# Decoding of all weight tiles but the first waits for the eighth pair's queries, and two more gates use Silu

## The chip, the cores and the metric

The kernel runs on one core of a Trainium2 chip. TensorE multiplies, VectorE and ScalarE work element by element, GpSimd does a little on the side, and SyncE issues the transfers. The metric is the device time of one execution in microseconds (us), as the median of several runs.

## What is computed

The inputs are q, k, v of 8 batches and 8 heads (576 tokens of 64 values), a projection to 128 features, and three weight matrices, which arrive as 64-bit floats. Linear attention comes first, a gated feed-forward over all 4608 tokens behind it:

```python
def phi(x):
    proj = np.einsum('bhsd,df->bhsf', x, w_phi)
    proj = proj - np.max(np.abs(proj), axis=-1, keepdims=True)
    return np.concatenate([np.exp(proj), np.exp(-proj)], axis=-1)
q_p, k_p = (phi(q), phi(k))
kv = np.einsum('bhsf,bhsd->bhfd', k_p, v)
z = np.sum(k_p, axis=2)
num = np.einsum('bhsf,bhfd->bhsd', q_p, kv)
den = np.einsum('bhsf,bhf->bhs', q_p, z)[..., None] + 1e-06
x = (num / den) ...                     # (4608, 512)
g = x @ w_gate                          # (4608, 1536)
silu = g * (1.0 / (1.0 + np.exp(-g)))
val = x @ w_val
return (silu * val @ w_out)
```

## The kernel before

The attention works on 32 pairs of heads, one after the other (`attention(i, rank)`). For each pair the keys are projected by TensorE, centred by VectorE (L498, L503), put through the exponential by ScalarE and multiplied with the values. The queries of the first eight pairs, the early ones, are projected, centred in three pieces (a maximum at L622, a subtraction at L627, whose three results are kept in `last["qm", n]`, n = 3i to 3i+2), turned on TensorE (L637) and exponentiated (L644). Their results are split into a rounded part and a remainder, `xh` and `xl` (L783, L785), the operands of the feed-forward. The sums of keys and values are copied by ScalarE at L561.

The feed-forward's inner width of 1536 is cut into 12 weight tiles f, the tokens into column tiles c of 384. For a weight tile and a column tile, `first` makes gate and value in two banks `gv` with 24 matmuls of 128x384 (4 blocks of the contraction, gate and value, 3 products of split operands), and `second` multiplies the result with w_out, 9 matmuls of 128x512. Weight tile after weight tile meets the first three column tiles, since these are done first; the products of column tiles 2 and 3 are stored and multiplied with w_out later. `first` makes the gate in two ways. With Tanh, ScalarE reads the gate's bank and VectorE reads it again (L878) before it multiplies with the value (L881). With Silu, ScalarE alone reads the gate's bank (L869), and VectorE makes one instruction (L872). Which one is taken is set by `SILU`, a half-open range of pairs (f, c).

The weights are decoded by `weight_piece`, once for the gate and value columns of a tile (`layer` 0, 128x1024, tiles named `a` or `spare`) and once for its rows of w_out (`layer` 1, 128x512, tiles named `spare` or `m`). A piece is loaded into one of three buffers. ScalarE takes the magnitude of the high words (L383), VectorE makes six steps of bit work and arithmetic (L384, L386, L389, L392, L394, L397), ScalarE rounds (L399), and VectorE makes the remainder (L400). The buffer of the raw words is free again after the fifth of VectorE's steps (L394). In the third buffer, `spare`, lie the w_out rows of tiles 0 and 1, and then the gate and value columns of tiles 3, 5, 7 and so on; gate and value columns of tiles 0, 1, 2, 4, 6 use the first.

The order of the instructions on all engines comes from a planner (`Plan`), which runs the steps in a model of the five engines when the program is built: each step has a cost, the steps that it follows, and a rank, and an engine that is free takes the ready step of the lowest rank. Attention of pair i has rank i, the feed-forward -1, the decoding 5 for the first piece and 7.12 to 7.33 for the others. When TensorE has nothing ready in the model, the planner writes a fill matmul on zeros (L1499 early, L1502 once a w_out sum is open), which it costs at 200 ns. On the chip every engine follows the written order.

Of the kernel before, what the change touches and what calls it, by code (L numbers as in the profile page):

```python
# [10 lines left out]
F32 = mybir.dt.float32  # L11
F32R = mybir.dt.float32r
U32 = mybir.dt.uint32
AF = mybir.ActivationFunctionType
# [13 lines left out]
NFT = DFF // P  # L28
# [16 lines left out]
EARLY_PAIRS = 8  # L45

W_RANKS = [5 if u == 0 else 7.125 if u == 1 else 7.1 + 0.01 * u for u in range(2 * NFT)]
SILU = (1, 0), (NFT - 3, 2)

EARLY = 3  # L50
PAIRS = 4
# [19 lines left out]
class Plan:  # L71
# [18 lines left out]
    def add(self, eng, cost, fn, after=(), rank=0.0, take=None, give=None):  # L90
        s = Step(eng, cost, fn, rank, len(self.steps), self.LAG[eng], take, give, (rank, len(self.steps)))
        seen = set()
        for a in after:
            if a is not None and id(a) not in seen:
                seen.add(id(a))
                a.then.append(s)
                s.left += 1
        s.early = self.early
        self.steps.append(s)
        return s  # L100
# [99 lines left out]
def dve(n):  # L200
    return 150 + 1.04 * n


def dve2(n):
    return 150 + 0.52 * n
# [6 lines left out]
def act(n):  # L212
    return 190 + 0.86 * n
# [11 lines left out]
def favor_attention_moe(ctx: ExitStack, tc: tile.TileContext, qT, kT, v, w_phi, wg, wv, wo, out):  # L225
    nc = tc.nc
# [13 lines left out]
    def sb(name, shape, dtype=F32, n=None):  # L240
        if n is None:
            return pool.tile(shape, dtype, name=name, tag=name)
        return [pool.tile(shape, dtype, name=f"{name}{i}", tag=f"{name}{i}") for i in range(n)]
# [52 lines left out]
    qm, qu = sb("qm", [P, 2 * NBL]), sb("qu", [P, 2 * NBL])  # L296
# [51 lines left out]
    add = plan.add  # L348
# [13 lines left out]
    raw_free, we_free, wa_free = [None] * 3, [None] * 3, [()] * 3  # L362

    def weight_piece(f, layer, rank, over):

        vec, n = nc.vector, (2 - layer) * DM
        u = (1 if f >= MORE else 2) if layer else (2 if f > MORE and f % 2 else 0)
        if f == MORE and layer:
            raw_free[1] = over
        first_ = lambda t: get(t)[:, :n]  # L370
        r = lambda: get((raw1, raw2, raw3)[u])[:, :2 * n].rearrange("p (n t) -> p n t", t=2)
        x, e = (lambda: first_((wa1, wa2, wa3)[u])), (lambda: first_((we1, we2, we3)[u]))
        low, high = (lambda: r()[:, :, 0]), (lambda: r()[:, :, 1])
        bits = lambda t: t.bitcast(U32)
        t = w1[f % W1_SETS]
        hi, lo = (w2_hi[f], w2_lo[f % W2_SETS]) if layer else (t[:, :, 0], t[:, :, 1])
        out_ = lambda x: x if layer else x.rearrange("p (u c) -> p u c", u=4)
        sets = (W1_SETS, W2_SETS)[layer]
        free = lo_user[layer][f - sets] if f >= sets else ()
        loads = [add("SP", (SLOW if f < 1 else INPUT) * P * DM * 8, lambda m=m, src=src: nc.sync.dma_start(  # L380
            get((raw1, raw2, raw3)[u])[:, 2 * DM * m:2 * DM * (m + 1)], src.bitcast(U32)), [raw_free[u]], rank)
            for m, src in enumerate([wo[f * P:(f + 1) * P]] if layer else [wg[f], wv[f]])]
        s0 = add("ACT", act(n), lambda: nc.scalar.activation(e(), high().bitcast(F32), AF.Abs), [*loads, we_free[u]], rank)  # L383
        s1 = add("DVE", dve2(n), lambda: vec.tensor_scalar(  # L384
            out=e(), in0=e(), scalar1=F64_LEAST, scalar2=F64_MOST, op0=ALU.max, op1=ALU.min), [s0], rank)
        s2 = add("DVE", dve2(n), lambda: vec.tensor_scalar(  # L386
            out=bits(e()), in0=bits(e()), scalar1=3, scalar2=0x3FFFFFFF, op0=ALU.logical_shift_left, op1=ALU.bitwise_and),
                 [s1], rank)
        s3 = add("DVE", dve(n), lambda: vec.scalar_tensor_tensor(  # L389
            out=bits(x()), in0=high(), scalar=0xC0000000, in1=bits(e()), op0=ALU.bitwise_and, op1=ALU.bitwise_or),  # L390
            [s2, *wa_free[u]], rank)
        s4 = add("DVE", dve2(n), lambda: vec.tensor_scalar(  # L392
            out=bits(e()), in0=bits(x()), scalar1=0xFF800000, scalar2=None, op0=ALU.bitwise_and), [s3], rank)
        s5 = add("DVE", dve(n), lambda: vec.scalar_tensor_tensor(  # L394
            out=e(), in0=low(), scalar=2.0**-52, in1=e(), op0=ALU.mult, op1=ALU.mult), [s4], rank)
        raw_free[u] = s5
        s6 = add("DVE", dve(n), lambda: vec.tensor_tensor(out=x(), in0=x(), in1=e(), op=ALU.add), [s5], rank)  # L397
        we_free[u] = s6
        s7 = add("ACT", act(n), lambda: nc.scalar.copy(hi, out_(x())), [s6, *(() if layer else free)], rank)  # L399
        s8 = add("DVE", dve(n), lambda: vec.tensor_tensor(out=lo, in0=out_(x()), in1=hi, op=ALU.subtract),  # L400
                 [s7, *free], rank)
        wa_free[u] = [s8]
        w_ready[f, layer] = [s7, s8]
        if not layer:
            w_stored[f, 4] = add("SP", P * n * 4, lambda: nc.sync.dma_start(w1_whole[f], x()), [s6], rank)
            wa_free[u].append(w_stored[f, 4])
        if layer:
            w_stored[f, layer] = add("SP", P * n * 4, lambda: nc.sync.dma_start(w2_dram[f], lo.bitcast(F32)), [s8], rank)
            w_stored[f, 4 + layer] = add("SP", P * n * 4, lambda: nc.sync.dma_start(w2_whole[f], x()), [s6], rank)
            wa_free[u].append(w_stored[f, 4 + layer])  # L410
        else:
            store = lambda x, f=f, t=t: w_stored.update({(f, 0): add("SP", P * n * 8, lambda: nc.sync.dma_start(
                w1_dram[f, :, :4], t.rearrange("p u h c -> p u (h c)").bitcast(F32)), [s8, x], rank)})
            if f:
                while later:
                    later.pop()(s8)
                store(None)
            else:
                later.append(store)
        if f == NFT - 1:  # L420
            weights_done.append(s8)
# [12 lines left out]
    last = {}  # L434
# [403 lines left out]
    def first(c, f, low):  # L838
# [28 lines left out]

        if c < EARLY and SILU[0] <= (f, c) < SILU[1]:
            s1 = add("ACT", act(CH), lambda: nc.scalar.activation(get(t_), ps_gv[0][:, :CH], AF.Silu),  # L869
# [90 lines left out]
    for f in range(NFT):  # L960
        for layer in range(2):
            weight_piece(f, layer, W_RANKS[2 * f + layer], over)
        low = parts_of_weights(f, 0, w_ready[f, 0])
        for c in range(EARLY):
            if c == EARLY - 1 and f == NFT - 1:
                put_off()
            j, h = first(c, f, low)
            if c:
                keep(c, f, j, h)
            else:  # L970
                put_off(0, f, parts(j, h), parts_of_weights(f, 1, w_ready[f, 1]))
# [40 lines left out]
    s0, s1_ = ((set2 + n) % X_SETS for n in (1, 2))  # L1012
# [541 lines left out]
```

## Time and profile before

| | |
|---|---|
| time, median of 3 runs (lowest, highest) | 1138.6 us (1135.88, 1138.96) |
| profiled execution: time, span | 1135.21 us, 1133.3 us |
| TensorE clock granted, mean | 0.997 |
| busy: TensorE, VectorE, ScalarE, GpSimd | 99%, 78%, 55%, 9% |
| TensorE on the chain that ended last | 88% |

The span goes from the first to the last instruction. Busy shares are means over stages of different kinds: the early pairs of heads with the decoding between them up to about 107 us, the twelve weight tiles for three column tiles beside the rest of the decoding to about 240 us, and after that the other pairs and column tiles.

### The profile page before, as it was taken

The numbers are of one execution on the slowest core, as the hardware profiler recorded it, in microseconds if no ns is written. First come the engines' busy times: TensorE is split into PE (matmuls) and PEld (weight loads), VectorE is DVE, ScalarE is ACT, GpSimd is POOL, SyncE is SP. The second block draws the span as 40 slices with busy tenths as digits, with TensorE's granted clock in tenths as the row PEclk, the third lists the DMA queues.
The fourth block names the chain that finished last, engine by engine and source line by source line (L and its number), as shares of the span: only waits on it lengthen the run. The fifth ranks groups of instructions, "written<-read, shape, count | busy, mean of one in ns | idle before, by whom it ended". The sixth has DMA issues, their size and how long they took to land.

```text
span 1133.3 us, 28130 instructions
## 1 busy us (share of the span) xinstructions
PE 1116.4 (99%) x11185; PEld 1061.5 (94%) x11185; DVE 889.3 (78%) x1418; ACT 627.6 (55%) x1373; POOL 104.3 (9%) x192
## 2 busy tenths in 40 slices
PE   9998999999999999999999999999999999999998
PEld 8887999999888899999899999999999999999998
DVE  6989999888787878889888999858556567979663
ACT  6876433365667676676675765644334345444342
POOL 0000000012120222122101000000420000000000
PEclk9999999999999999999999999999999999999999
DMA  6656899754788887789888897689997888642511
GB/s 176 170 186 231 300 315 297 259 178 139 233 256 256 275 267 257 242 282 328 263 254 262 288 351 248 222 257 325 306 305 235 266 263 288 212 167 85 182 43 42
DMA packets 161554, 269.56 MB, mean 238 GB/s; under 512 B 56464, under 2 KB 106640, under 8 KB 158352
## 3 DMA queue, kind: packets, MB, share of 16 engines
q1 hardware_dynamic: 161120, 267.64, 72.4%
q8 instruction: 88, 1.44, 0.5%
q14 instruction: 42, 0.34, 0.1%
q10 hardware_dynamic: 304, 0.13, 0.0%
HBM read 187.50 MB, written 80.22 MB: 236 GB/s over the span
## 4 chain that ended last, share of the span: by engine, by line
PE 88%; DMA 4%; DVE 4%; ACT 1%; issue 1%; POOL 0%; ACTq 0%; SPq 0%; DVEq 0%; POOLq 0%
PE gv L357 18%; PE gv L1127 14%; PE o L1127 14%; PE o L357 9%; PE work L1374 7%; PE work L357 5%; PE gv L1374 5%; PE o L1374 5%; PE work L540 4%; PE work L727 4%; DMA w<-w_dram 2%; PE work L767 1%; PE work L549 1%; DMA a<-w_dram 1%; DMA w_dram<-a 1%
## 5 line engine op out<-in xcount | busy, mean ns | idle before, releaser
L357 PE MATMUL gv<-xh,w 128*128 128x384 f32 x768 | 212.6, 341 | 1.1 <-DVE m L878 0.6
L357 PEld LDWEIGHTS gv<-xh,w 128*128 128x128 f32 x768 | 140.2, 188 | 3.5 <-DVE m L878 1.1
L357 PE MATMUL gv<-xl,w 128*128 128x384 f32 x384 | 128.9, 336 | 0.0
L357 PE MATMUL o<-w_hi,hidden 128*128 128x512 f32 x288 | 102.7, 402 | 0.0
L1127 PE MATMUL gv<-xh,w 128*128 128x384 f32 x336 | 99.8, 340 | 2.5 <-DMA w<-w_dram 1.5
L1127 PE MATMUL o<-m,w 128*128 128x384 f32 x388 | 80.9, 336 | 0.3 <-ACT snap L1137 0.2
L357 PEld LDWEIGHTS gv<-xl,w 128*128 128x128 f32 x384 | 72.3, 188 | 1.0 <-DVE xl L785 0.3
L1127 PEld LDWEIGHTS o<-m,w 128*128 128x128 f32 x388 | 68.5, 188 | 1.0 <-ACT snap L1137 0.6
L1127 PEld LDWEIGHTS gv<-xh,w 128*128 128x128 f32 x336 | 61.8, 188 | 4.4 <-issue 3.0
L357 PEld LDWEIGHTS o<-w_hi,hidden 128*128 128x128 f32 x288 | 54.1, 188 | 10.9
L1140 DVE TENSOR_TENSOR snap<-o,snap 128x384 f32<-128x384 f32 x72 | 39.9, 555 | 28.3 <-PE o L1127 23.3
L1140 DVE TENSOR_TENSOR snap<-gv,snap 128x384 f32<-128x384 f32 x72 | 39.9, 554 | 26.7 <-PE gv L1127 18.4
L1137 ACT COPY snap<-gv 128x384 f32<-128x384 f32 x72 | 34.3, 476 | 42.8 <-PE gv L1127 26.6
L357 PE MATMUL o<-w_lo,hidden 128*128 128x512 f32 x144 | 56.9, 395 | 0.0
L1137 ACT COPY snap<-o 128x384 f32<-128x384 f32 x72 | 34.2, 476 | 40.9 <-PE o L1127 25.2
L1127 PE MATMUL o<-xh,w 128*128 128x384 f32 x188 | 55.6, 341 | 1.0 <-DMA w<-w_dram 1.0
L1127 PE MATMUL gv<-xl,w 128*128 128x384 f32 x168 | 56.4, 336 | 0.0
L1147 ACT ACTIVATE m<-snap 128x384 f32<-128x384 f32 x47 | 24.7, 525 | 53.2 <-DVE snap L1140 47.5
L498 DVE TENSOR_REDUCE km<-work 128x4 f32<-128x512 f32 (+1 forms) x85 | 46.6, 548 | 8.8 <-PE work L357 8.6
L727 PE MATMUL work<-m,m 128*64 128x65 f32 x1664 | 53.4, 221 | 0.0
L727 PEld LDWEIGHTS work<-m,m 128*64 128x64 f32 x1664 | 51.0, 138 | 0.2 <-issue 0.2
L980 POOL TENSOR_TENSOR m<-m 128x256 f32<-128x256 f32 x48 | 38.6, 803 | 128.6 <-ACT m L528 26.3
(448 smaller groups left out, 3080.1 us busy)
## 6 DMA issues: line engine op xcount, KB each, us to landing
w<-w_dram SPq DMA_DIRECT2D x113, 512.0 KB, 5.6
h_dram<-m SPq DMA_DIRECT2D x90, 192.0 KB, 5.0
w_dram<-w SPq DMA_DIRECT2D x12, 1024.0 KB, 6.4
w_dram<-a SPq DMA_DIRECT2D x24, 512.0 KB, 4.1
w<-w_dram SPq DMA_DIRECT2D x12, 1024.0 KB, 7.4
w<-w_dram SPq DMA_DIRECT2D x38, 256.0 KB, 4.0
w_lo<-w_dram SPq DMA_DIRECT2D x36, 256.0 KB, 3.9
spare<-h_dram SPq DMA_DIRECT2D x19, 384.0 KB, 4.3
```

The source lines that it names most:

```text
L357: nc.tensor.matmul(o, l, r, start=a, stop=z)
L498: kmax = add("DVE", dve(n * NF), lambda m=m, view=view: vec.tensor_reduce(out=m, in_=view(), axis=AX.X, op=ALU.max, apply_absolute_value=T ...
L540: nc.tensor.matmul(o[c, n:n + D2], kp[h][:, t, k, c], get(vf[one])[:, t, h], start=t + k == 0, stop=False)
L549: nc.tensor.matmul(work[plan.bank[names[h]]][c, n:n + D2], kp[2][r, 0, k, c], get(vf[one])[r, 4, h], start=False, stop=k == 1)
L727: nc.tensor.matmul(o[c * D:(c + 1) * D, t * D2:(t + 1) * D2], (qe, qx)[k][j][:, h, n:n + D], kvs[j][:, (2 * h + k) * D2:(2 * h + k + 1) * D2],
L767: nc.tensor.transpose(o[:, m * P:(m + 1) * P], x, ident)
L980: done = [add("POOL", POOLED, lambda o=o, l=l, r=r: gp.tensor_tensor(out=x(o), in0=x(l), in1=x(r), op=ALU.subtract), done, rank)]
L1127: nc.tensor.matmul(o[:, :CH], l, r, start=begin and i == 0, stop=i == len(terms) - 1, skip_group_check=True)
L1137: return add("ACT", act(CH), lambda: act_.copy(snap[n], bank[:, :CH]), [after, *snap_free[n]], FIRST)
L1140: return add("DVE", dve(CH), lambda: vec.tensor_tensor(out=snap[n], in0=bank[:, :CH], in1=snap[n], op=ALU.add), after, FIRST)
L1147: t0 = add("ACT", act(CH), lambda: act_.activation(get(t_), get(x), AF.Tanh, scale=0.5), [*after, th_free[j]], FIRST)
L1374: nc.tensor.matmul(cut(o, t - ts[0], W), l, r, start=begin and q == 0 and m == 0 and t == ts[0], stop=q == NQ - 1 and m == 2, skip_group_c ...
```

## The change

All pieces but the first wide one (`f or layer` is true for them) get a further step that their first instruction, the magnitude at L383, follows: the last of the eighth pair's three query centrings. The loads don't wait for it. And `SILU` begins at (0, 1), so that column tiles 2 and 3 of the first weight tile use Silu; the first column tile of it keeps Tanh.

```diff
-SILU = (1, 0), (NFT - 3, 2)
+SILU = (0, 1), (NFT - 3, 2)
...
-        s0 = add("ACT", act(n), lambda: nc.scalar.activation(e(), high().bitcast(F32), AF.Abs), [*loads, we_free[u]], rank)
+        s0 = add("ACT", act(n), lambda: nc.scalar.activation(e(), high().bitcast(F32), AF.Abs), [*loads, we_free[u], last["qm", 3 * EARLY_PAIRS - 1] if f or layer else None], rank)
```

The planner makes a new order of this. On VectorE, around the eighth pair's query centrings, stood before (`km` are the maxima, `m5` the centred queries, `spare` the first w_out rows being decoded):

```order
L503 TENSOR_TENSOR m1_0_83<-work0_109,km2_89 128x4x128
L394 SCALAR_TENSOR_TENSOR spare_100<-spare_100 128x512
L498 TENSOR_REDUCE km3_90<-o2_106 128x1
L503 TENSOR_TENSOR m1_0_83<-o2_106,km3_90 128x128
L397 TENSOR_TENSOR spare_100<-spare_100 128x512
L622 TENSOR_REDUCE km1_88<-o1_105 128x4
L627 TENSOR_TENSOR m5_0_85<-o1_105,km1_88 128x512
```

There stand now on VectorE, up to the third centring and to the first step of decoding behind it (`a2` is the second tile's gate and value columns):

```order
L622 TENSOR_REDUCE km1_88<-work0_109 128x4
L627 TENSOR_TENSOR m5_0_85<-work0_109,km1_88 128x512
L622 TENSOR_REDUCE km2_89<-work1_110 128x4
L627 TENSOR_TENSOR m5_0_85<-work1_110,km2_89 128x512
L622 TENSOR_REDUCE km3_90<-o1_105 128x1
L627 TENSOR_TENSOR m5_0_85<-o1_105,km3_90 128x128
L748 RECIPROCAL rc0_94<-rc0_94 128x9
L751 TENSOR_TENSOR m2_0_84<-work2_111,rc0_94 128x4x64
L751 TENSOR_TENSOR m2_0_84<-o0_104,rc0_94 128x4x64
L785 TENSOR_TENSOR xl1_81<-o0_104,xh1_78 128x192
L785 TENSOR_TENSOR xl2_82<-work1_110,xh2_79 128x384
L384 TENSOR_SCALAR a2_0_102<-a2_0_102 128x1024
```

The decoding of the second gate and value piece and of the first w_out rows, which stood between the sixth, seventh and eighth pairs on VectorE, now all stands behind the last centring.

On VectorE, at the third weight tile's last column tile (its gate is the L872 on `th_96`) and the fourth weight tile's gate and value columns (`spare_100`, 128x1024, made into `w10_72`), stand now:

```order
L400 TENSOR_TENSOR w11_73<-a2_0_102,w11_73 128x4x256
L872 SCALAR_TENSOR_TENSOR th_96<-th_96,gv1_108 128x384
L384 TENSOR_SCALAR spare_100<-spare_100 128x1024
L386 TENSOR_SCALAR spare_100<-spare_100 128x1024
L389 SCALAR_TENSOR_TENSOR spare_100<-spare_100 128x1024
L392 TENSOR_SCALAR spare_100<-spare_100 128x1024
L394 SCALAR_TENSOR_TENSOR spare_100<-spare_100 128x1024
L397 TENSOR_TENSOR spare_100<-spare_100 128x1024
L389 SCALAR_TENSOR_TENSOR m3_1_1609<-m3_1_1609 128x512
L392 TENSOR_SCALAR m3_1_1609<-m3_1_1609 128x512
L394 SCALAR_TENSOR_TENSOR m3_1_1609<-m3_1_1609 128x512
L400 TENSOR_TENSOR w10_72<-spare_100,w10_72 128x4x256
```

The L400 at the top is the last step of the fifth weight tile's gate and value columns, which now come ahead of the fourth's. Before, the fourth's last step stood ahead of all three gates of the third weight tile. From the last `xl` (L785) of the early pairs to the L872 on `th_96` in this piece VectorE has 48 instructions: the w_out rows of tiles 0 to 2 whole and two steps of tile 3's, the gate and value columns of tiles 2 and 4 whole and the last step of tile 1's, eight gates (L872) and two splits (L902).

On TensorE, between the third weight tile (`w12_74`) and the fourth (`w10_72`), stand now:

```order
L357 MATMUL gv1_108<-xl2_82,w12_74 128x384
L357 MATMUL gv1_108<-xh2_79,w12_74 128x384
L1502 MATMUL o0_104<-nil_112 128x256 x48
L357 MATMUL gv0_107<-xh0_77,w10_72 128x384
L357 MATMUL gv0_107<-xl0_80,w10_72 128x384
```

The 48 fills are new; before, the fourth weight tile followed the third directly. The 27 early fills (L1499) are the same; six fills (L1502) that stood much later, near 246 us of the profile, are gone.

## Rows read from the trace of the kernel before

**Rows 1.** Busy time by stretch: us; PE, PEld, DVE, ACT, POOL (instructions); clock; DMA share.

```profile
50.00:88.40 38.40, 35.61 (x633) 31.74 (x630) 34.24 (x72) 29.27 (x86) 0.00 (x0) 0.96 0.63 203
106.70:141.00 34.30, 33.65 (x187) 32.52 (x187) 32.77 (x50) 14.28 (x21) 0.00 (x0) 1.00 0.91 312
141.00:230.00 89.00, 89.00 (x495) 86.56 (x495) 81.51 (x119) 32.19 (x50) 0.33 (x3) 1.00 0.83 281
```

**Rows 2.** Who TensorE waited for after 141 us: us in total, times, longest.

```profile
PE gv L1127 <- DMA w<-w_dram: 1.5, 3, 0.7
PE gv L1127 <- DMA h_dram<-m: 1.0, 1, 1.0
```

**Rows 3.** Timeline of TensorE, 54 to 112 us: start, us, instruction, [idle before, releaser].

```profile
57.31 0.58 PE L357 MATMUL o<-wst,m 64*128 64x128 f32 x1 [2.25 <-ACT m L561]
...
99.78 0.33 PE L767 MATMUL o<-ident,m 128*128 128x128 f32 x1 [1.18 <-DVE m L751]
...
101.08 0.45 PE L357 MATMUL gv<-xh,w 128*128 128x384 f32 x1 [0.46 <-ACT xh L783]
...
111.66 0.45 PE L357 MATMUL gv<-xh,w 128*128 128x384 f32 x1 [0.65 <-DVE m L878]
```

**Rows 4.** Busy time by stretch again; the clock is the third number from the end.

```profile
57.30:60.70 3.40, 3.39 (x42) 3.17 (x44) 3.09 (x7) 3.37 (x13) 0.00 (x0) 0.50 0.11 13
101.67:105.07 3.40, 3.40 (x50) 2.97 (x52) 3.37 (x6) 1.40 (x3) 0.00 (x0) 0.50 0.62 186
```

**Rows 5.** Timeline of ScalarE, 54 to 58 us.

```profile
55.39 1.12 ACT L383 ACTIVATE a<-a 128x1024 f32<-128x1024 f32 x1 [1.57 <-DMA a<-in_wv_dram]
...
56.98 0.45 ACT L561 COPY m<-o 128x130 f32<-128x130 f32 x2
```

**Rows 6.** Groups of VectorE's instructions by form, 50 to 240 us: busy us, mean ns.

```profile
L389 DVE SCALAR_TENSOR_TENSOR m<-m 128x512 uint32<-128x512 uint32 x10 | 6.9, 691 | 0.3
...
L389 DVE SCALAR_TENSOR_TENSOR spare<-spare 128x1024 uint32<-128x1024 uint32 x5 | 6.1, 1221 | 0.1
...
L384 DVE TENSOR_SCALAR m<-m 128x512 f32<-128x512 f32 x10 | 4.2, 421 | 0.0
...
L384 DVE TENSOR_SCALAR spare<-spare 128x1024 f32<-128x1024 f32 x5 | 3.4, 686 | 0.0
```

**Rows 7.** Timeline of VectorE: last query centring of pairs 2, 5 and 8.

```profile
20.37 0.28 DVE L627 TENSOR_TENSOR m<-gv,km 128x128 f32<-128x128 f32 x1
...
50.60 0.28 DVE L627 TENSOR_TENSOR m<-o,km 128x128 f32<-128x128 f32 x1
...
88.12 0.28 DVE L627 TENSOR_TENSOR m<-o,km 128x128 f32<-128x128 f32 x1
```

**Rows 8.** Timeline of TensorE, end of the fourth weight tile's first column tile.

```profile
144.82 0.33 PE L357 MATMUL gv<-xl,w 128*128 128x384 f32 x1
145.00 0.34 PE L357 MATMUL gv<-xh,w 128*128 128x384 f32 x1
```

**Rows 9.** Timeline of VectorE: last step of the fourth tile's gate and value columns.

```profile
122.98 1.22 DVE L400 TENSOR_TENSOR w<-spare,w 128x1024 fp32r<-128x1024 f32 x1
```

**Rows 10.** Groups by form, 50 to 240 us: the gate on VectorE, the cast on ScalarE.

```profile
L872 DVE SCALAR_TENSOR_TENSOR m<-m,gv 128x384 f32<-128x384 f32 x19 | 10.5, 552 | 6.1 <-PE gv L357 5.1 <-ACT w L399 0.5
...
L399 ACT CAST w<-spare 128x1024 fp32r<-128x1024 f32 x5 | 5.3, 1051 | 3.4 <-PE gv L357 2.8 <-DVE spare L397 0.6
```

**Rows 11.** The six late fills on TensorE: timeline, and their group.

```profile
245.88 0.87 PE L1502 MATMUL o<-nil 128*128 128x256 f32 x6
...
L1502 PE MATMUL o<-nil 128*128 128x256 f32 x6 | 0.9, 280 | 0.0
```

**Rows 12.** Timeline of TensorE: 64 small matmuls at full and at half clock.

```profile
51.71 2.09 PE L540 MATMUL o<-m,m 128*64 128x65 f32 x64
...
102.45 3.28 PE L540 MATMUL work<-m,m 128*64 128x65 f32 x64
```

**Rows 13.** Timelines of SyncE and ScalarE: loads of the fourth tile's piece, and its first step.

```profile
102.98 0.33 SPq L380 DMA_DIRECT2D spare<-in_wg_dram  x1
...
110.91 1.11 ACT L383 ACTIVATE spare<-spare 128x1024 f32<-128x1024 f32 x1
```

## The prediction

> **What bounds the kernel now.** I read the split by cores first, then the clock and busy times by stretch, then who waited for whom, then the timeline of single engines. TensorE is busy 99% of the span, and from 141 to 230 us all of it [rows 1]; the matmuls follow each other without a gap there, so every microsecond that TensorE gains or loses before 141 us is handed on to the end. The longest single wait after 141 us is 1.0 us [rows 2]. The change is therefore read in the first 141 us, up to the first matmul of the fourth weight tile. There VectorE is nearly as full as TensorE: 34.24 of 38.40 us from 50 to 88.4, 32.77 of 34.30 from 106.7 to 141 [rows 1]. What TensorE loses there is few waits: 2.25 us at 55 us, where ScalarE's copy `m` (L561) came late; 1.18, 0.46 and 0.65 us between 98 and 112 [rows 3]. Behind the first and the second of these the granted clock is 0.50, TensorE's lower level, for 3.4 us each [rows 4]. The 2.25 us are of the decoding's making: ScalarE stood 1.57 us before the Abs of the second wide piece, whose data had not landed, then ran it for 1.12 us, and the copy stood behind it [rows 5].
>
> I call the gate and value columns of weight tile n its wide piece (128x1024), the rows of w_out its narrow piece (128x512). A wide piece costs VectorE three steps of 0.69 and four of 1.22 us, 6.95 in all; a narrow one three of 0.42 and four of 0.69, 4.03 [rows 6].
>
> **Part 1: what leaves the attention of the early pairs.** Between the last centring of the fifth pair's queries (50.60) and that of the eighth's (88.12) VectorE now runs the second wide and the first narrow piece; after the change no row of either stands there (first two pieces of order shown above). How much sooner does the eighth pair get there? From below and above by the pace. The second pair's last centring lies at 20.37, the fifth's at 50.60, the eighth's at 88.12 [rows 7]: 30.2 us for three pairs with the first wide piece among them, 10.1 a pair, and then 37.5 for three. Three pairs at 10.1 would be 30.3, so 7.2 us sooner. But TensorE has the first column tile's 24 matmuls among those three pairs, before and after, and none among the earlier ones; matmuls of this form start 0.18 us apart [rows 8], so they take some 4.2 us, and with these wholly on the path 3.0 us are left. Neither engine alone is the limit there, so I take the middle, 5.1. From 88.4 to 106.7 little is won, because now the second wide piece is decoded there where the third was.
>
> **Part 2: Silu for the first weight tile's column tiles 2 and 3.** Tanh needs a second pass on VectorE that reads the gate's bank (L878), and TensorE waited 0.65 us for it at 111.66 [rows 3]. Silu frees the bank from ScalarE; 0.65 is won. Two VectorE instructions of 0.55 us go, in a stretch where VectorE is not ahead of TensorE, so nothing more is counted. ScalarE's program has three table loads before and after; the one to Silu moves ahead of the first weight tile's second column tile and still comes behind the last early exponential: nothing.
>
> So TensorE reaches the end of the third weight tile 5.1 + 0.65 = 5.8 us sooner, at about 135.2 instead of 141.0. Bounds: 3.0 and, if the waits of 1.18 and 0.46 also go, 7.2 + 0.65 + 1.64 = 9.5.
>
> **Part 3: the new wait.** Before, the fourth wide piece is ready at 122.98 + 1.22 = 124.2 [rows 9], 16.8 us ahead of its first matmul (141.0, 23 starts of 0.174 us before that at 145.00 [rows 8]). After, it is late, and the order says by how much. The third buffer (`spare`) holds first narrow piece 1, then narrow piece 2, and only then wide piece 4, so wide piece 5, in another buffer, is decoded ahead of it. VectorE takes its instructions in the order written, and there the gate of the third weight tile's last column tile (L872 on `th`) stands before the first step of wide piece 4. That gate waits for the last matmul of weight tile 3, so the whole decoding follows TensorE's last matmul: gate 0.55, six steps 3 x 0.69 + 3 x 1.22 = 5.73, then L389, L392, L394 of a narrow piece, 0.69 + 0.43 + 0.69 = 1.81, which cover ScalarE's cast of 1.05, and the last step 1.22 [rows 6, 10]: 9.3. Is VectorE at that gate in time? From the last `xl` to the gate it has 48 instructions: narrow pieces 1 to 3 (12.1), wide pieces 3 and 5 (13.9), the last step of wide piece 2 (1.2), two steps of the next narrow piece (0.85), eight gates and two splits of 0.55 (5.5), together 33.6 [rows 6, 10]. TensorE was busy 33.65 us in the same stretch of before [rows 1]. So it is about in time; I add 0.3 us for that and take 9.6. What is queued behind the gate on TensorE is 48 fill matmuls and then the whole weight tile 4.
>
> Six fills took 0.87 us where the clock was full, the last one's 0.28 included [rows 11], so they start 0.12 us apart: 48 take 5.7 us, inside the wait. They cost nothing while the wait is longer. What is left of the wait, 3.9 us, is idle, and after idle stretches of 2.25 us and of 1.18 and 0.46 us the clock fell [rows 3, 4]. At 0.50, 64 small matmuls of L540 took 3.28 us, at full clock 2.09 [rows 12]: 1.2 us lost in one half-clock stretch. A dense stretch of 3.4 us at half speed loses up to 1.7. I take 1.3. The Trainium skill, page "TensorE: Matmul & The Clock Gate", section Terms, puts the penalty at the throttled time times one minus the granted share: 1.7 us, by which the sum below would be 0.4 us higher; the stretch of small matmuls shows less than that.
>
> **Part 4: the rest.** Six fills at 245.88 (0.87 us [rows 11]) are gone from the order; they may have covered a wait, so I count half, 0.4. The steps behind are ordered anew to the end, with the same work; with single waits of 1.0 us at most there now, I allow 2 us either way. Loads are not later than their use: the second wide piece lies in its buffer long before.
>
> **Sum.** -5.8 + 9.6 + 1.3 - 0.4 = +4.7 us. The profiled execution took 1135.2 (span 1133.3), 3.4 under the median of the three runs, 1138.6; against its own time the sum gives 1139.9, against the median 1143.3.
>
> **Rivals.**
> The head start pays for the wait. Place: 50 to 107 us. With 9.5 us gained, the sum is -9.5 + 9.6 + 1.3 - 0.4 = +1.0, 1139.6. For it: the pace of 10.1 us a pair was reached with a wide piece in it. Against it: the extra 24 matmuls, and the chain behind the last centring (transposes, exponentials, sums, scaling) that has waits of its own.
>
> VectorE alone is the limit of the early pairs (faster). Then all steps that leave it are won: 6.95 + 4.03 less the last narrow step 0.69 = 10.3, and with 0.65 and 1.64 as above 12.6. If the fills also keep the clock, the sum is -12.6 + 9.6 - 0.9 = -3.9, 1134.7. It decides from 12.1 us of head start on. For it: VectorE was busy 34.24 of 38.40 us. Against it: TensorE was busy 35.61 there [rows 1], and it must still do the same matmuls.
>
> The fourth wide piece is later still. Its loads wait for the fifth step of narrow piece 2; from there to the gate VectorE has 18 instructions, 13.3 us. From the first such load's issue (102.98) to its Abs (110.91) it was 7.9 us before [rows 13]. So 5.4 us are in hand; but SyncE's queue has stores ahead of these loads that wait for gates. Late by 3 us beyond that: 1146.3 and more.
>
> The change does not do what it says: excluded by the order, where the steps have moved.
>
> **How the numbers follow.** 0.3% is 3.4 us, about what a measurement of this kernel can tell from no change: slower begins at 1142.0, faster ends at 1135.2. My case (a wait that outweighs the head start, 1140 to 1147): 0.60, of which 0.50 lie above 1142.0. Head start pays for it: 0.22. VectorE alone: 0.10. Later still: 0.08. So slower 0.58, same 0.32, faster 0.10. The range goes from 1136.5 (the second case less 2 us of reordering, and one more for the tail toward the third) to 1147.5 (a head start of 3.0, -3.0 + 9.6 + 1.7 = +8.3, 1146.9, and half a microsecond for a late gate).
>
> **What would show it.** Right: the eighth pair's last centring at 82 to 84 us; no wait for L561 of 2 us near 55 us; 48 fills of L1502 near 135 us and behind them 3 to 4 us of idle TensorE ended by VectorE's `w` (L400); the clock at 0.50 after that; from there on all times of before plus about 5 us. Wrong: fills that end where the piece is already ready; a first matmul of weight tile 4 before 140 us; or new waits of several microseconds after 230 us, in the reordered remainder, which I hold at 2.

## The result and the profile after

The changed kernel takes 1151.4 us (median of 4 runs, 1150.1 to 1155.0) against 1137.2 for the kernel before in the same comparison: ratio 1.013, 95% interval 1.010 to 1.017, so 11 to 19 us slower. I had predicted slower, at 1143.3 with a range to 1147.5: the direction was right, the size was not, and the time lies outside the range. The profiled execution took 1155.0 us (span 1153.2, granted clock 0.991) and is the slowest of the four; that of before took 1135.2 (span 1133.3), 2.0 under its median. So the two traces lie 19.9 us apart, the medians 14.2.

The page's row of TensorE, to be held against the 99% of before:

```profile
PE 1126.4 (98%) x11227; PEld 1071.6 (93%) x11227; DVE 886.0 (77%) x1416; ACT 625.7 (54%) x1373; POOL 112.6 (10%) x192
```

Timeline of VectorE in the changed kernel: the eighth pair's last centring, the first and the last of the six steps of wide piece 2 (on `a`), the last `xl` of the early pairs, and the place of the new wait.

```profile
83.60 0.29 DVE L627 TENSOR_TENSOR m<-o,km 128x128 f32<-128x128 f32 x1
...
89.45 0.69 DVE L384 TENSOR_SCALAR a<-a 128x1024 f32<-128x1024 f32 x1 [2.29 <-ACT a L383]
...
98.78 1.23 DVE L397 TENSOR_TENSOR a<-a 128x1024 f32<-128x1024 f32 x1
99.93 0.81 DVE L785 TENSOR_TENSOR xl<-o,xh 128x192 fp32r<-128x192 f32 x2
...
139.75 0.56 DVE L872 SCALAR_TENSOR_TENSOR th<-th,gv 128x384 f32<-128x384 f32 x1 [1.68 <-PE gv L357]
140.22 0.69 DVE L384 TENSOR_SCALAR spare<-spare 128x1024 f32<-128x1024 f32 x1
...
147.85 1.22 DVE L400 TENSOR_TENSOR w<-spare,w 128x1024 fp32r<-128x1024 f32 x1
```

The centring answers to [rows 7]: 83.60 instead of 88.12. The L872 on `th` and the L384 behind it are the pair on which the prediction rested: the gate of the third weight tile stands ahead of the first step of wide piece 4, which is ready at 149.1.

Timeline of ScalarE in the changed kernel, around the first gates and at the third weight tile's end:

```profile
101.00 0.27 ACT L561 COPY m<-work 128x130 f32<-128x130 f32 x1
101.28 1.28 ACT L869 ACT_TABLE_LOAD   x1
102.57 0.49 ACT L869 ACTIVATE m<-gv 128x384 f32<-128x384 f32 x1
...
135.33 1.05 ACT L399 CAST w<-a 128x1024 fp32r<-128x1024 f32 x1 [0.79 <-DVE a L397]
137.60 0.49 ACT L869 ACTIVATE th<-gv 128x384 f32<-128x384 f32 x1 [1.21 <-DMA a<-in_wg_dram]
137.98 1.11 ACT L383 ACTIVATE spare<-spare 128x1024 f32<-128x1024 f32 x1
146.18 1.05 ACT L399 CAST w<-spare 128x1024 fp32r<-128x1024 f32 x1 [7.08 <-DVE spare L397]
...
167.35 0.49 ACT L869 ACTIVATE th<-gv 128x384 f32<-128x384 f32 x1 [0.20 <-PE gv L357]
```

Timeline of ScalarE in the kernel before, the gates that answer to those at 137.60 and 167.35:

```profile
139.13 0.49 ACT L869 ACTIVATE th<-gv 128x384 f32<-128x384 f32 x1 [1.46 <-PE gv L357]
...
158.61 0.48 ACT L869 ACTIVATE th<-gv 128x384 f32<-128x384 f32 x1
```

The row at 137.60 is the third weight tile's last gate. TensorE leaves that tile 1.9 us behind its start in the changed kernel and in the one before, so it dates the work of TensorE and is a good mark for comparing kernels. (The page puts the idle time before it down to a load; in the run with the burst moved, below, the same 1.21 us are put down to TensorE's `gv`.) I use it below as "mark 3" (before: 139.13), and the same gate of weight tile 4 as "mark 4" (before: 158.61; changed kernel: 167.35). The cast at 135.33 is wide piece 5's; piece 4's magnitude (137.98) and cast (146.18) come only behind it.

Timeline of TensorE in the changed kernel, with the idle time ahead of an instruction and what ended it:

```profile
100.33 0.44 PE L357 MATMUL gv<-xl,w 128*128 128x384 f32 x1 [1.46 <-DVE xl L785]
103.12 0.69 PE L357 MATMUL gv<-xh,w 128*128 128x384 f32 x1 [1.65 <-ACT m L869]
...
139.48 5.90 PE L1502 MATMUL o<-nil 128*128 128x256 f32 x48
147.28 0.44 PE L357 MATMUL gv<-xh,w 128*128 128x384 f32 x1 [1.90 <-ACT w L399]
149.12 0.66 PE L357 MATMUL gv<-xh,w 128*128 128x384 f32 x2 [1.23 <-DVE w L400]
...
881.82 0.66 PE L1127 MATMUL gv<-m,w 128*128 128x384 f32 x1 [4.69 <-DMA w<-w_dram]
```

The new wait runs from 139.48 to 149.12, 9.6 us, with the 48 fills in it and, at 147.28, the first two matmuls of weight tile 4, which need only what ScalarE rounded. The last row is something that the prediction did not have. Busy time by stretch (the clock is the third number from the end) for the stretches behind 101.8, behind the new wait, and behind that late wait:

```profile
101.80:108.60 6.80, 5.48 (x17) 5.49 (x18) 4.45 (x7) 2.42 (x3) 0.00 (x0) 0.50 1.03 341
...
149.60:153.00 3.40, 3.40 (x12) 3.40 (x11) 3.33 (x6) 1.11 (x2) 0.00 (x0) 0.50 1.05 407
881.80:886.80 5.00, 4.98 (x16) 5.00 (x17) 0.69 (x2) 1.51 (x3) 0.00 (x0) 0.50 0.94 376
```

After 141 us before had no single wait over 1.0 us [rows 2]. The changed kernel's list of waits there (us in total, times, longest) begins:

```profile
PE gv L1127 <- DMA w<-w_dram: 4.7, 1, 4.7
PE o L1127 <- DMA w<-w_dram: 2.3, 3, 1.4
PE o L1127 <- DVE snap L1140: 2.2, 1, 2.2
```

So the loss is in two lumps. Mark 3 is 1.5 us early, mark 4 is 8.7 us late. The late wait is 4.69 us, and 5.0 us of gapless work at half clock behind it lose up to another 2.5: 7.2 together. The span is 19.9 us longer; 19.9 - 8.7 - 7.2 leaves 4.0 us, about what the 2.2 us wait for `snap` (at 600) and the 3.4 us of half clock behind it come to. Timeline of SyncE's queue in the changed kernel, ahead of the late wait:

```profile
864.60 0.38 SPq L1060 DMA_DIRECT2D w<-w_dram  x1
865.08 6.11 SPq L1239 DMA_DIRECT2D spare<-w_whole  x9
871.29 0.38 SPq L888 DMA_DIRECT2D h_dram<-m  x1
871.71 1.39 SPq L1239 DMA_DIRECT2D spare<-w_whole  x3
873.15 0.43 SPq L1236 DMA_DIRECT2D spare<-w_sums  x1
873.67 1.00 SPq L1060 DMA_DIRECT2D w<-w_dram  x2
```

The kernel's second half multiplies by blocks whose weights are loaded just ahead of use into slots (L1060; first, second and third slot are `w_72`, `w_73` and `w_74`, and buffer `a` holds one more). In one place it also issues a burst: 12 loads of 128 KB (L1239) and one of 768 KB (L1236). The changed kernel's order has this burst between the load of the second slot (864.60) and those of the third (873.67), which are issued 9.1 us after it and land too late for 877.1, where TensorE begins to wait. Before has the burst (843.4 to 851.4) further ahead, behind the second load of the first slot (839.75), with the loads of `a` and of the second and third slot behind it, and no such wait. Timeline of SyncE's queue in the kernel before:

```profile
839.75 0.94 SPq L1060 DMA_DIRECT2D w<-w_dram  x1
...
843.40 6.01 SPq L1239 DMA_DIRECT2D spare<-w_whole  x10
...
850.92 0.44 SPq L1236 DMA_DIRECT2D spare<-w_sums  x1
851.46 0.38 SPq L1060 DMA_DIRECT2D a<-w_dram  x1
...
852.40 1.55 SPq L1060 DMA_DIRECT2D w<-w_dram  x2
```

### The profile page after: what moved, and what is told of

Same layout as the page of the kernel before. It is cut to its first block, busy times and chain, and to the rows that moved or that the text cites. A ratio compares the mean times of both kernels' runs of the same rounds, so it can differ in the third digit from the quotient of the medians.

```text
span 1153.2 us, 28213 instructions
## 1 busy us (share of the span) xinstructions
PE 1126.4 (98%) x11227; PEld 1071.6 (93%) x11227; DVE 886.0 (77%) x1416; ACT 625.7 (54%) x1373; POOL 112.6 (10%) x192
## 4 chain that ended last, share of the span: by engine, by line
PE 85%; DMA 7%; DVE 4%; ACT 2%; issue 1%; SPq 1%; POOL 0%; DVEq 0%; ACTq 0%; POOLq 0%
PE gv L357 16%; PE o L1127 13%; PE gv L1127 12%; PE o L357 9%; PE work L1374 7%; PE work L357 5%; PE gv L1374 4%; PE o L1374 4%; PE work L540 4%; PE work L727 4%; DMA w<-w_dram 3%; DMA w_dram<-a 2%; PE work L767 1%; PE o L540 1%; PE work L549 1%
## 5 line engine op out<-in xcount | busy, mean ns | idle before, releaser
L357 PEld LDWEIGHTS gv<-xh,w 128*128 128x128 f32 x768 | 142.6, 191 | 8.4 <-ACT m L869 2.3
L1127 PEld LDWEIGHTS gv<-xh,w 128*128 128x128 f32 x336 | 62.4, 189 | 1.3 <-ACT snap L1137 1.0
L980 POOL TENSOR_TENSOR m<-m 128x256 f32<-128x256 f32 x48 | 41.8, 871 | 90.6 <-DMA m<-w_whole 79.4
```

Source lines behind the costliest of these rows:

```text
L357: nc.tensor.matmul(o, l, r, start=a, stop=z)
L980: done = [add("POOL", POOLED, lambda o=o, l=l, r=r: gp.tensor_tensor(out=x(o), in0=x(l), in1=x(r), op=ALU.subtract), done, rank)]
L1127: nc.tensor.matmul(o[:, :CH], l, r, start=begin and i == 0, stop=i == len(terms) - 1, skip_group_check=True)
```

## Experiments

All times are medians. The runs come in four groups, each on another chip and each beside runs of the kernel before, whose medians were 1136.3, 1136.6, 1137.4 and 1137.4; ratios are taken within a group. Diffs are against the changed kernel, unless it is said otherwise.

**Once more, unchanged.**

> The changed kernel once more, nothing edited. If the late waits of its first profile (PE o on a snap copy, 2.2 us at 600; PE gv on a weight load from memory, 4.7 us at 880, each with a half-clock stretch behind it) come from the order of the instructions, both stand at the same places again and the time is 1150 to 1155 us. If they are chance of one execution, the profile has neither, its span is about 5 to 7 us below 1153.2, and lost time behind weight tile 4 stays at +10 to +11 against before to the end.

Measured: 1153.6 us (ratio 1.015, 1.014 to 1.017). The wait for the weight load at 878 is there again (4.8 us) and 6.8 us of half clock behind it; the 2.2 us wait at 600 is not. So the late wait belongs to the order, the other was chance. The changed kernel has now two medians, 1151.4 and 1153.6; where a run is compared with it, both count.

**The wait alone, and the Silu alone.**

```diff
-SILU = (0, 1), (NFT - 3, 2)
+SILU = (1, 0), (NFT - 3, 2)
```

> The wait without the earlier Silu (column tiles 2 and 3 of weight tile 1 keep tanh). Theory A, the table load in the tail costs the head start: the 1.65 us wait of column tile 3 for the gate bank and the 6.8 us of half clock from 101.8 go back to before's 3.4 us or less, the third weight tile ends at 135 to 136 instead of 139.5, and the time is 3 to 5 us below the changed kernel's. Theory B, the pieces that now stand among the eighth pair's last casts and the first gates cost it: the third weight tile ends at 138.5 to 140.5 and the time is within 1.5 us of the changed kernel's. Under both the wait for wide piece 4 stays at 8 to 13 us, since nothing of it is changed.

Measured: 1147.1 us (1.010, 1.008 to 1.011), mark 3 at 138.65. The tail of the early pairs (84 to 107 us) is no faster without the table load: where the changed kernel waits 1.65 us for L869, this one waits 1.7 for L878, and the half clock of 6.8 us is there too. Theory A falls for the tail. But 6.4 us against the changed kernel in the same group came back elsewhere, more than either theory had; the second run without Silu, below, finds the place.

```diff
- ... [*loads, we_free[u], last["qm", 3 * EARLY_PAIRS - 1] if f or layer else None], rank)
+ ... [*loads, we_free[u], None], rank)
```

> The earlier Silu without the wait. Theory A: the table load, now at about 102.6, holds the gate bank 1.3 us longer in front of column tile 3; 2 to 5 us slower than before, 1139 to 1142. Theory B: as priced in the prediction, 0.65 us won in three gates and a load that costs nothing or 1.3 us once: 1136 to 1139, the same as before.

Measured: 1135.7 us (0.999, 0.998 to 1.001), 0.6 below before. Theory B, as priced; the loss needs the wait.

**Only gate and value pieces wait; then only w_out pieces.**

```diff
- ... last["qm", 3 * EARLY_PAIRS - 1] if f or layer else None], rank)
+ ... last["qm", 3 * EARLY_PAIRS - 1] if f and not layer else None], rank)
```

> Only gate and value pieces wait for the eighth pair's centring; the w_out pieces (narrow pieces) do not. Theory C, the 9.6 us before weight tile 4 come from the buffer: narrow pieces 1 and 2 hold the one that wide piece 4 loads into, so its load is issued 21 us later; here narrow 1 and 2 are decoded early, wide piece 4 loads before 105 and TensorE waits under 2 us in front of weight tile 4; time 8 to 11 us below the changed kernel's, 1140 to 1144. Theory D, VectorE simply has more decoding to do after 84 than time: the wait stays, 6 us or more (it has 2 narrow pieces of about 4.2 us of VectorE less to do there), and the time is within 4 us of the changed kernel's.

Measured: 1141.8 us (1.005, 1.004 to 1.006). TensorE does not wait in front of weight tile 4; mark 3 is at 138.22, mark 4 at 156.99. What is left over before is the late wait, 5.0 us, and its 6.8 us of half clock.

```diff
- ... last["qm", 3 * EARLY_PAIRS - 1] if f or layer else None], rank)
+ ... last["qm", 3 * EARLY_PAIRS - 1] if layer else None], rank)
```

> The mirror of the run in which gate and value pieces wait: only the w_out pieces wait for the eighth pair's last centring, gate and value pieces do not; the earlier Silu stays. Theory C, narrow pieces 1 and 2 hold the buffer of wide piece 4: though no wide piece is put off, TensorE waits in front of weight tile 4, 2 to 8 us at 138 to 147. Theory D, the wait came of VectorE's total of decoding behind 84: with only three or four narrow pieces put off (about 4.2 us of VectorE each) and all wide ones in time, there is no wait over 1 us there. The burst of 12 loads stands at 840 to 849 ahead of the load for the second slot, as in the run that waits for the sixth pair, so theory E wants a wait of 4 to 5 us for a weight load at about 855 under both: 1141 to 1148 under D, 2 to 8 us more under C.

Measured: 1146.5 us (1.008, 1.006 to 1.011), no wait in front of weight tile 4 either. Theory C, as I had put it, falls: the w_out pieces in the third buffer do not make the wait by themselves. Timeline of VectorE in this kernel, the last step of wide piece 4:

```profile
125.89 1.22 DVE L400 TENSOR_TENSOR w<-spare,w 128x1024 fp32r<-128x1024 f32 x1
```

That is 22 us sooner than in the changed kernel, with only half of the pieces let go. What sets the changed kernel apart from both is the order of pieces 4 and 5: ScalarE's cast of piece 5 (135.33) comes ahead of that of piece 4 (146.18). With only the w_out pieces waiting, piece 4's cast is at 124.75 and piece 5's at 131.69; where only the wide ones wait (the kernel of that kind with the burst moved, below) at 125.74 and 138.68. Both kinds together bring the buffer so late (piece 4's load is issued at 124.31, piece 5's at 115.26) that the planner takes piece 5 first. With only the w_out pieces waiting it is 110.22 against 118.21. Neither theory C nor theory D names this.

**The burst moved in the changed kernel, and in the kernel before.** A planner step without an instruction, 7 us long in the model, ahead of the burst. It leaves TensorE's order as it was, and that of the other engines up to the burst:

```diff
+        hold = add("POOL", 7000, lambda: None, [x for y in stage_free for x in y], NEXT)
         for n in range(3):
-            pieces_read.append(piece_of_weights(n, ..., [x for y in stage_free for x in y],
+            pieces_read.append(piece_of_weights(n, ..., [hold, *(x for y in stage_free for x in y)],
```

> The changed kernel, with the burst of 12 loads of 128 KB (the first piece of the summed output weights, behind the sixth tile's blocks at 865) placed behind the two loads of the third slot's gate and value weights instead of between them and the load ahead of them; no work is added or left out. Theory E, that burst is what the single late wait is for (4.7 us at 877 and 6.8 us at half clock behind it): the wait is gone, lost time between 850 and 900 is under 2 us instead of 6 to 7, and the time falls by 5 to 7 us, to 1146 to 1149. Theory F, any order has such a wait somewhere because the memory is loaded to 99% there: another wait of 3 us or more comes within 30 us and the time stays within 2 us of the changed kernel's.

Measured: 1146.4 us (1.009, 1.007 to 1.011), 5.1 and 7.2 below the two medians of the changed kernel. Theory E, and by about the size read from the trace (7.2). SyncE's queue in this kernel:

```profile
862.00 0.90 SPq L1060 DMA_DIRECT2D w<-w_dram  x2
865.27 0.32 SPq L888 DMA_DIRECT2D h_dram<-m  x1
865.64 0.42 SPq L1060 DMA_DIRECT2D w<-w_dram  x1
868.91 0.32 SPq L888 DMA_DIRECT2D h_dram<-m  x1
869.28 5.78 SPq L1239 DMA_DIRECT2D spare<-w_whole  x10
```

All three loads are now ahead of the burst; between 852 and 885 TensorE has no wait. In the kernel before the same edit with 8000 puts the burst where the change has it:

> The kernel before, with that burst moved later, to the place that it has in the changed kernel: between the load for the second slot and those for the third. Nothing else is edited and nothing is left out. Theory E: a PE wait for a weight load of 4 to 5 us appears at about 860, with half clock behind it, and the time is 5 to 7 us above before's, 1141 to 1144. Theory F: within 2 us of before's.

Measured: 1140.9 us (1.004, 1.002 to 1.006), 4.3 above before. TensorE's timeline in this kernel:

```profile
871.83 0.41 PE L1127 MATMUL gv<-m,w 128*128 128x384 f32 x1 [2.46 <-DMA w<-w_dram]
```

The wait appears, at 2.5 us instead of 4.7, and without half clock behind it. So the place of the burst is a cost by itself, below the 5 to 7 expected. How large it is here the trace does not show: this execution (1143.3) has another 5.3 us of waits for weight loads, but they lie at 600 to 840, ahead of the burst, where the order is that of the kernel before.

**Both repairs together.** Only gate and value pieces wait, and the burst is moved by 7000:

> The wait for gate and value pieces only, with the burst behind the third slot's loads. Theories C and E add: wide_wait's 1141.8 less its 7.4 us between 850 and 875, 1134 to 1136, so 0 to 2 us faster than before. If the two causes do not add (theory F), 1140 to 1142.

Measured: 1133.2 us (0.996, 0.994 to 0.998): 2 to 6 us faster than before. The two effects add; the time is a little below the 1134 to 1136 expected.

**Only wide piece 2 waits, and for the sixth pair.**

```diff
- ... last["qm", 3 * EARLY_PAIRS - 1] if f or layer else None], rank)
+ ... last["qm", 17] if (f, layer) == (1, 0) else None], rank)
```

> Of the decode only wide piece 2 waits, and for the sixth pair's last centring (63.9 in before's profile) instead of the eighth's; the earlier Silu stays. Theory G: ScalarE no longer stands at 55 in front of a load that has not landed, the 2.0 to 2.3 us wait of TensorE at 57 is gone, nothing is put off far enough to be late at weight tile 4, and the burst stays ahead of the second slot's load; 1 to 3 us faster than before, 1133 to 1136. Against it: the 2 us are given back before 141 as in the changed kernel's tail, 1136 to 1138.

Measured: 1144.4 us (1.008, 1.005 to 1.010), a miss. Index 17 is the sixth pair's last centring. The first half of theory G holds: the wait for L561 is gone, and mark 3, by ScalarE's timeline, is the earliest of all orders, 4.6 us ahead of before:

```profile
134.56 0.49 ACT L869 ACTIVATE th<-gv 128x384 f32<-128x384 f32 x1 [3.05 <-PE gv L357]
```

The other half does not: the order has the burst ahead of a load into `a`, and by TensorE's timeline of this kernel that is paid for there.

```profile
856.19 0.66 PE L1127 MATMUL gv<-m,a 128*128 128x384 f32 x1 [4.48 <-DMA a<-w_dram]
```

With the burst moved behind by 6000:

> Only wide piece 2 waits, for the sixth pair's last centring, with the earlier Silu; and the burst goes back behind the second load for the first slot, where the kernel before has it. Theory E: the 4.5 us wait for a weight load at 852 to 856 and the 6.8 us of half clock behind it go, lost time between 825 and 875 is 1 to 2 us instead of 7, and the time falls by 6 to 9 us against the kernel without that, to 1135 to 1138. Theory F, the memory is full there in any order: 1142 to 1146.

Measured: 1140.4 us (1.002, 1.001 to 1.004), 4.0 less. This lies between the two theories. That wait goes (1.5 us are the most for a load into `a`), but a wait of 3.2 us for another slot and a half-clock stretch stand in this profile at 790, ahead of the burst, where the run before this one waits 2.6 us. The profile is of the fastest of twelve executions (1137.0), and the 4.6 us of head start are not found at the end. Where the rest of them is spent is open.

**The whole wait without Silu, burst moved.** As the wait alone, with 7000:

> The whole wait without the earlier Silu, with the burst of 12 loads behind the third slot's loads. Theory E: a wait for a weight load of 4.6 us at 869 and its half clock go, 5 to 7 us off the 1147.1 of the whole wait without the earlier Silu: 1140 to 1142. Theory A', the earlier Silu adds its own loss to the whole wait (1153.6 against 1147.1 in one call): it stands 4 to 7 us below the 1146.4 of the same kernel with the earlier Silu. If that difference came from the places of the burst, it stands within 2 us of 1146.4.

Measured: 1140.9 us (1.004, 1.002 to 1.005), 5.4 below the same kernel with the earlier Silu, in another group; within one group the pair with the burst unmoved gave 6.4. Theory A' is right that the Silu costs this much beside the whole wait; the place is the new wait. VectorE's timeline in this kernel:

```profile
137.26 1.23 DVE L389 SCALAR_TENSOR_TENSOR spare<-spare 128x1024 uint32<-128x1024 uint32 x1
139.51 0.56 DVE L872 SCALAR_TENSOR_TENSOR th<-th,gv 128x384 f32<-128x384 f32 x1 [1.01 <-PE gv L357]
139.98 0.69 DVE L392 TENSOR_SCALAR spare<-spare 128x1024 uint32<-128x1024 uint32 x1
```

TensorE's timeline in the same kernel, from the first fill to the end of the wait:

```profile
139.24 4.58 PE L1503 MATMUL o<-nil 128*128 128x256 f32 x37
144.32 0.44 PE L357 MATMUL gv<-xh,w 128*128 128x384 f32 x1 [0.50 <-ACT w L399]
...
146.16 0.61 PE L357 MATMUL gv<-xh,w 128*128 128x384 f32 x2 [1.23 <-DVE w L400]
```

Here three steps of wide piece 4 (0.69, 0.69, 1.23) stand ahead of the gate, and the wait is 139.24 to 146.16, 6.9 us: 2.7 less than 9.6, about those 2.6. Behind it the clock does not fall. In the kernel with Silu and the burst moved it does, by the busy times of the stretch:

```profile
147.40:154.10 6.70, 6.08 (x19) 6.08 (x20) 4.90 (x7) 1.12 (x2) 0.00 (x0) 0.50 0.98 383
```

From mark 3 to mark 4 that kernel takes 167.48 - 136.50 = 31.0 us, this one 162.83 - 137.35 = 25.5. Of the difference, 5.5, 2.7 are the wait; I put the other 2.8 down to the clock. The changed kernel, with 3.4 us at half clock there, takes 167.35 - 137.60 = 29.8: 2.7 for the wait and 1.6 for the clock.

**The faster kernel without the earlier Silu.** As with both repairs, but `SILU = (1, 0)` and 14000, which gives the burst the same place:

> As the kernel that beat before (gate and value pieces wait, burst behind the third slot's loads), but column tiles 2 and 3 of weight tile 1 keep tanh. Theory A': the table load no longer stands in front of column tile 3's gate bank, the 1.6 us wait for it goes and the time falls by 1 to 6 us from 1133.2. Theory B (Silu saves 0.65 us in three gates and its load costs at most what it saves): 1132 to 1135, the same.

Measured: 1131.5 us (0.994, 0.992 to 0.996). It is 1.7 below the kernel with Silu, but the intervals overlap; whether Silu costs anything there is not settled. Its trace has waits for L878 (2.2 us in two) where the other has 1.6 us for L869, so the expected gain in the tail is not seen.

## Why the prediction was off

**Part 1, the head start.** The time to the last centring was right (83.60, within 82 to 84; 4.5 us sooner, 5.1 predicted), and the wait for L561 near 55 us is gone. What failed is the sentence that from 88.4 to 106.7 little is won. There 2 to 3 us are lost: mark 3 is 1.5, 2.7 and 2.6 us ahead in three executions of this order (the changed kernel, its repeat, the run with the burst moved), not 5.8. VectorE runs the six steps of wide piece 2 among the chain to the last `xl` (89.45 to 99.93), and TensorE waits 1.46 us for that `xl` and 1.65 for the gate; behind them it runs 6.8 us at half clock in the profile above (3.4 in the two others), against 3.4 before [rows 4]. With wide piece 2 released by the sixth pair instead, the head start is 4.6 at mark 3, in an execution without any half clock before it; what the release gave and what the clock is not separated. The Silu alone, without the wait, is 2.4 ahead at mark 3 (136.70, without the half clock at 57). So nothing is left there that must be the wait's.

**Part 2, Silu.** By itself as priced, within the noise (0.6). The table load was counted at nothing; it took 1.28 us between L561 and the first Silu, and TensorE waited behind it 1.65 us, but with Tanh it waited there too, 1.7 us in one execution of that order and 0.9 in another, and mark 3 came no sooner. What was missed is that the earlier Silu also moves wide piece 4's first three steps behind the gate: 5.4 to 6.4 us with the whole wait.

**Part 3, the new wait.** Right in mechanism and size: 48 fills, 0.12 us apart (5.90 in all), 9.6 us, ended by L400. The run with three steps ahead of the gate shortened it by their length, which shows the mechanism. The clock's price, 1.3, was nearly right for the changed kernel, where the comparison above gives 1.6, and too low for the run with the burst moved, where it gives 2.8; the length of the half clock (3.4 and 6.8 us) differs between executions of the same order. The 64 small matmuls from which I took the price lie only 2.6 us inside their half-clock stretch [rows 4, 12], so they show less than a whole one. The Trainium skill, "TensorE: Matmul & The Clock Gate", section Terms, puts the penalty at the throttled time times one minus the granted share. By that the 3.4 us behind the changed kernel's wait cost 1.7, and the 6.1 us from the end of the other's wait (148.0) to 154.1 at 0.50 cost 3.1, close to the 1.6 and 2.8 found above.

**Part 4, the rest.** "I allow 2 us either way" is the step that failed most, and with it "Loads are not later than their use", which I had read for one load only. The burst's new place costs 5.1 to 7.2 us by the medians, 7.2 in the trace; without that the change takes 1146.4, inside the range. I had named new waits of several microseconds in the reordered remainder as what would prove me wrong, and read no place of SyncE's order there. The second step that failed is the head start: the sum has mark 4 late by 9.6 + 1.3 - 5.8 = 5.1 us, and it was 8.7, 7.4 and 8.9 late in the three executions. With the burst's 5.1 to 7.2 that makes 12.5 to 16.1, against the 14.2 and 17.3 that the two medians show.

By medians the whole runs, the first three in one group: 1136.6 before, -3.4 for letting only the wide pieces wait with the burst out of the way, +13.2 for letting the w_out pieces wait too, and +5.1 to +7.2 for the burst. Without the earlier Silu, in another group, letting the w_out pieces wait too costs some 9.5 (1131.5 to 1140.9). The +13.2 is larger than mark 4 shows (167.48 against 157.06, 10.4); the last 3 us of it are not placed.

**Rivals.** The head start did not pay, VectorE alone was not the limit (the last centring came 4.5 us sooner, not 10.3), and the fourth piece's load was not late: its magnitude came at 137.98, directly behind the gate's Silu.

## What to carry to other kernels

Where a planner writes the order, an edit at the start can change the order of loads 700 us later: lay the queue's order before and after side by side over the whole program, and look for bursts that have changed places with loads of near use. Where work is made to wait, look for where it goes instead: here wide piece 2 went from the early pairs into the chain to the last `xl`, and the head start was spent there. A head start early on need not reach the end: the order in which only wide piece 2 waits, some 4.6 us ahead at mark 3, took 1140.4 us with the burst moved, and the one in which all wide pieces wait for the eighth pair, 0.8 ahead there, took 1133.2. And two delays of which neither alone makes TensorE wait in a place (here weight tile 4) can do so together, when they turn the order in which two pieces are decoded.

## What the hardware showed unexpectedly

Nearly the same stall does not always cost the clock. Before, 2.25 us of idle TensorE at 55 us are followed by 3.4 us at 0.50 [rows 3, 4]; with the Silu alone, whose order is the same up to there, the stall is 2.04 us and the clock stays at full behind it. TensorE's timeline of that kernel:

```profile
56.97 0.37 PE L357 MATMUL o<-wst,m 64*128 64x128 f32 x1 [2.04 <-ACT m L561]
```

Busy times of the stretch behind that wait:

```profile
57.00:60.40 3.40, 3.40 (x89) 3.18 (x89) 3.33 (x8) 3.37 (x13) 0.00 (x0) 1.00 0.31 83
```

Those two stalls differ by 0.2 us, and whether that decides is not shown. But the 9.6 us wait with its 48 fills was followed by 3.4 us at half clock in two executions (the changed kernel and its repeat) and by 6.8 in a third whose order is the same up to there (the burst moved). The 6.9 us wait with 37 fills was followed by none, in both executions of that order.
